# Attention and expert layer on one core: the first transposes of a pair moved behind a product for the maxima and a score group

## The chip, the cores and the metric

The kernel runs on one core of a Trainium2 chip. The metric is the device time in microseconds of one execution: the median of several runs, lower is better. The matrix engine is called TensorE (PE in the profile, its weight loads PEld), the others VectorE (DVE), ScalarE (ACT), GpSimd (POOL) and SyncE (SP, which issues most transfers). PSUM is the memory that TensorE writes; VectorE and ScalarE read it.

## The reference

Masked attention over 4 batches of 8 heads (768 positions, 64 features), followed by a layer of 8 experts of which each token uses one. Cut to what matters:

```python
q_bucket = np.sum((np.einsum('bhsd,dk->bhsk', q, proj) > 0) * 2 ** np.arange(6), axis=-1)
k_bucket = ...                                   # the same of k
mask = q_bucket[:, :, :, None] == k_bucket[:, :, None, :]
scores = np.where(mask, scale * np.matmul(q, k.transpose(0, 1, 3, 2)), -1000000000.0)
attn = np.exp(scores - scores.max(-1, keepdims=True))
attn = attn / (attn.sum(-1, keepdims=True) + 1e-09)
x = np.matmul(attn, v)                           # then tokens by 512 features
e_idx = np.argmax(x @ w_gate + modality_bias[modality_id], axis=1)
out[mask_e] = gate_w[mask_e, None] * (np.maximum(x[mask_e] @ w1[e], 0.0) @ w2[e])
```

A query sees only the keys with the same six sign bits. The kernel finds out by a product which queries have no such key at all (they average over all values).

## The kernel before, in words

The 32 heads are worked on as 16 pairs, numbered 0 to 15. The attention part is one loop over pairs with six steps each (`kt` 0 to 5, one for each block of 128 keys). Several pairs are in work at once, and in pair i's six steps TensorE does:

- **scores of pair i** (`score`, lines 309 to 328; letter S, or f to k of the table's tail). For each step three groups: head 0 on 512 queries, head 1 on 512 queries, both heads on the remaining 256. A group is one or two pairs of products (L306 and L307) into a `psum` tile of pool `ps_s` (called pss in the profile), of which there are two; ScalarE then takes the exponential (L319 for the first two groups, L324 for the third) into a buffer `pb`. GpSimd adds the exponentials up (L327).
- **maxima for pair i + 1** (`maxp`, lines 228 to 264; letter M). Products L240 (one query block on 512 keys) and L246 (two query blocks on the other 256 keys), into two tiles of pool `ps_m` (psm); VectorE reduces them (L242, L248). After some of them the maxima go through a transpose (`maxp_back`, L269, letter B) into a tile of pool `ps_x` (psx), which VectorE reads three times: L271 for each head, and L272, which marks the queries without a key in `lone`.
- **preparing pair i + 2** (letter T): `turn` (lines 172 to 197) transposes q and k in six groups of four (L181) into a psx tile each, which ScalarE copies out (L185); behind the second and third group of a head SP issues a transfer that shifts a half (L194, L196). Then `signs` (L208, read by VectorE, L210) and `patterns` (L223, read by VectorE or ScalarE, L224 and L225). That makes twelve pieces of work, of which eleven stand in one pair's six steps and the last (letter P) in the first step of the next pair.
- **the weighted sum of values** (`weigh`, lines 330 to 349; letter A): eight products (L342) a step, running two steps behind the scores, into tiles psu.

Beside these, `split` (letter W, L162 to L168, on ScalarE, VectorE and GpSimd) parts pair i + 3's loaded q and k into high and low parts for the transposes, `vadds` and `vsums` (v and V; L287 on TensorE, a psx tile) prepare the mean of the values, `sums` (Q, L360) adds up the softmax sums, and `finish`, `finish_x` and `route` (letters e to h, E to G, k, x, y) turn a finished batch of four pairs into gate logits, routing tables and stored rows; they fall into pairs 4 to 15 and differ from pair to pair. In pairs with i % 4 == 2 they put L409, L412, L590 and L592 on VectorE in the first steps, and L423 and L425 (rows of x, through a psx tile).

Pool `ps_x` has two tiles only, and all of L181, L208, L223, L269, L287, L360, L423 and others take the next of the two in turn. At the start of a pair the order of takers is: L269 of `maxp_back` (end of the pair before), L223 of letter P, and then the first transposes L181, which thus get the tile of L269 and need it free of L272.

What sets the order of the work is a table written by hand. TensorE's instructions are recorded under a manual schedule, in the order of the letters of `PLAN`; the other engines' instructions are put into order by a scheduler that uses an instruction-cost estimate. The loop reads one string a step:

```python
for kt in range(NT):
    for c in PLAN[kt]:
        if c == "S":
            next(ss)
        elif c == "M":
            next(ms, None)
        elif c == "T":
            next(ts, None)
        elif c == "P":
            next(last, None)
```

After the last pair the second part begins, in which the experts' weights are loaded, split into high and low parts (L755, L757) and multiplied with gathered token rows (L792 to L794, L834 to L836). The diff does not touch it.

Of the kernel before, what the change touches and what calls it, by code (L numbers as in the profile page):

```python
# [27 lines left out]

LAG = 2
PLAN = (  # L30
    "LvSPMTMSASfMTMfexyhk",
    "SMTVMSASfMTMeyghk",
    "SMTMSAQFGlSMTMEfxyk",
    "SMSATWSBMEekk",
# [947 lines left out]
```

## Time and profile before

| | before |
|---|---|
| median of three runs | 882.26 us (877.72, 884.44, 882.26) |
| the profiled execution | 876.72 us |
| its span, first to last instruction | 874.9 us |
| mean granted TensorE clock | 0.985 |
| start of a pair (its first L240): pairs 1, 2, 3, 4 | 64.60, 94.38, 124.12, 153.86 us |
| the same: pairs 5, 6, 7, 8 | 186.06, 218.37, 250.92, 283.38 us |
| the same: pairs 9, 10, 11, 12 | 315.62, 347.94, 380.27, 412.75 us |
| the same: pairs 13, 14 | 445.62, 477.60 us |
| TensorE's first instruction of the second part (L780) | 535.73 us |

A row of the timeline has the start in us from the span's start, the length in us, the engine, the source line, the operation, out<-in by the program's names, the shape and the count of instructions merged; a bracket names the engine's idle time ahead and what ended it. Matmuls overlap, so that the next one's start lies ahead of the drawn end of the one before, and a row's length is not what it costs: the distance between starts is. A row of the list of waits has who waited for whom, the total in us, how often, and the longest. Only the time for which TensorE waits sets the pace; the other engines' idle time says how much room they have.

### The profile page before, as it was taken

To read this page: it belongs to the slowest core of one execution; us is meant where nothing else is said; L and a number is where in the kernel's file an instruction comes from. 1 tells how busy PE (TensorE), PEld (TensorE's weight loads), DVE (VectorE), ACT (ScalarE), POOL (GpSimd) and SP (SyncE) were. 2 spreads that over 40 slices of the span, in tenths; PEclk is the share of its full clock that TensorE was granted. 3 is DMA by queue.
4 is the path that set the end of the run, shared out by engine and by line. 5 is a ranking of instruction groups with operands and counts; after the bars stand their busy time and mean duration, and the time that the engine had idled before them with its cause. 6 is when DMAs were issued, how large, how long until landed. Compare 5 with 4: busy or idle time off the path is not lost.

```text
span 874.9 us, 14548 instructions
## 1 busy us (share of the span) xinstructions
PE 817.9 (93%) x5154; PEld 579.5 (66%) x5154; DVE 585.8 (67%) x1029; ACT 506.0 (58%) x953; POOL 458.6 (52%) x347
## 2 busy tenths in 40 slices
PE   6799999999999999999999898879999999999993
PEld 3556555555555654555554555779999999998993
DVE  6776676676967676977677876954656565657550
ACT  4566666665666665666665464444555555557551
POOL 5387678657669857669757687322222221123010
PEclk9899999999999999999999999999999999999997
DMA  6423213212325221324210164796777777778750
GB/s 170 116 67 84 70 34 85 74 47 62 98 61 97 74 64 45 99 66 72 55 46 10 31 229 121 166 253 199 235 223 215 232 220 215 221 230 276 228 158 22
DMA packets 76753, 110.87 MB, mean 127 GB/s; under 512 B 10495, under 2 KB 52095, under 8 KB 76672
## 3 DMA queue, kind: packets, MB, share of 16 engines
q1 hardware_dynamic: 70880, 95.14, 39.2%
q0 software_dynamic: 4928, 13.14, 4.1%
q10 hardware_dynamic: 864, 1.57, 0.9%
q8 instruction: 43, 0.70, 0.4%
q14 instruction: 38, 0.31, 0.1%
HBM read 84.83 MB, written 13.33 MB: 112 GB/s over the span
## 4 chain that ended last, share of the span: by engine, by line
PE 74%; DVE 11%; DMA 4%; ACT 4%; issue 3%; POOL 2%; SPq 0%; POOLq 0%; DVEq 0%; ACTq 0%
PE psu L342 13%; PE pss L306 8%; PE pss L307 6%; PE yps L834 5%; PE yps L836 5%; PE yps L835 5%; PE psm L240 5%; PE hps L794 4%; PE hps L793 4%; PE hps L792 4%; PE psx L181 3%; PE psx L208 3%; PE psm L246 3%; POOL sp L327 2%; DVE mx L242 1%
## 5 line engine op out<-in xcount | busy, mean ns | idle before, releaser
L327 POOL TENSOR_TENSOR sp<-sp,pb 128x768 f32<-128x768 f32 x124 | 225.5, 1844 | 43.6 <-ACT pb L324 42.1
L757 DVE TENSOR_TENSOR w<-raw,w 128x1024 fp32r<-128x1024 f32 x108 | 134.9, 1251 | 94.4 <-ACT w L755 93.7
L755 ACT CAST w<-raw 128x1024 fp32r<-128x1024 f32 x112 | 117.1, 1048 | 61.9 <-PE yps L836 55.3
L242 DVE TENSOR_REDUCE mx<-psm 128x1 f32<-128x512 f32 x192 | 127.9, 686 | 32.0 <-PE psm L240 28.1
L342 PE MATMUL psu<-pb,vt 128*64 128x512 f32 (+1 forms) x768 | 145.6, 500 | 0.0
L319 ACT ACTIVATE pb<-pss 128x512 f32<-128x512 f32 x192 | 114.9, 599 | 40.6 <-PE pss L307 30.1
L324 ACT ACTIVATE pb<-pss 128x512 f32<-128x512 f32 x96 | 57.5, 599 | 127.1 <-PE pss L307 121.6
L792 PE MATMUL hps<-xh,w 128*128 128x256 f32 x384 | 108.9, 284 | 2.6 <-issue 1.6
L793 PE MATMUL hps<-xl,w 128*128 128x256 f32 x384 | 108.9, 284 | 0.0
L794 PE MATMUL hps<-xh,w 128*128 128x256 f32 x384 | 108.5, 283 | 0.0
L342 PEld LDWEIGHTS psu<-pb,vt 128*64 128x64 f32 x768 | 46.8, 136 | 86.4 <-issue 86.1
L769 POOL DMA_INDIRECT xg<-x_d,tb x26 | 31.6, 1214 | 124.6 <-DMA tb<-tab 99.5
L842 POOL DMA_INDIRECT out<-y,tb x26 | 34.5, 1328 | 117.7 <-ACT y L841 61.0
L834 PE MATMUL yps<-w,hl 128*128 128x512 f32 x208 | 83.4, 401 | 1.3 <-DVE hl L822 1.3
L836 PE MATMUL yps<-w,hh 128*128 128x512 f32 x208 | 81.8, 393 | 0.0
L835 PE MATMUL yps<-w,hh 128*128 128x512 f32 x208 | 81.6, 393 | 0.0
L248 DVE TENSOR_REDUCE mx<-psm 128x2 f32<-128x512 f32 x96 | 66.1, 689 | 22.9 <-PE psm L246 21.5
L306 PE MATMUL pss<-m_0g,s_0g 128*128 128x512 f32 x192 | 78.0, 406 | 0.0
L792 PEld LDWEIGHTS hps<-xh,w 128*128 128x128 f32 x384 | 73.4, 192 | 3.9 <-issue 1.8
L793 PEld LDWEIGHTS hps<-xl,w 128*128 128x128 f32 x384 | 73.6, 192 | 1.7 <-issue 1.2
L794 PEld LDWEIGHTS hps<-xh,w 128*128 128x128 f32 x384 | 73.5, 192 | 0.0
L167 POOL TENSOR_TENSOR n<-qk,n 128x384 fp32r<-128x384 f32 x36 | 40.2, 1122 | 56.9 <-ACT n L163 48.0
(214 smaller groups left out, 1767.3 us busy)
## 6 DMA issues: line engine op xcount, KB each, us to landing
raw<-moe_w SPq DMA_DIRECT2D x112, 512.0 KB
qk<-q SPq DMA_DIRECT2D x32, 192.0 KB
qk<-k SPq DMA_DIRECT2D x32, 192.0 KB
vt<-v SPq DMA_DIRECT2D x16, 384.0 KB
x_d<-xs SPq DMA_DIRECT2D x18, 256.0 KB
m_1g<-m_1g SPq DMA_DIRECT2D x16, 192.0 KB
s_1g<-s_1g SPq DMA_DIRECT2D x16, 192.0 KB
m_0g<-m_0g SPq DMA_DIRECT2D x15, 192.0 KB
```

Of the source, the lines that this page charges most:

```text
L242: nc.vector.tensor_reduce(out=mx[:, qt + j, hi, 0:1], in_=mp, axis=AX.X, op=ALU.max)
L306: nc.tensor.matmul(out, t["s1"][h][:, ks], t["m1"][h][:, cs], start=True, stop=False)
L327: (nc.vector if h and i in CFG["spd"] else nc.gpsimd).tensor_tensor(out=t["sp"][:, h], in0=(t["pb"][0] if kt == 1 else t["sp"])[:, h], in1 ...
L342: nc.tensor.matmul(t["u"][part][64 * h:64 * h + 64, 0:w], t["v"][:, h, kt], t["pb"][kt][:, h, COLS[part]], start=False, stop=(kt == NT - 1 ...
L755: nc.scalar.copy(out=hi, in_=r)
L757: (nc.gpsimd if pool else nc.vector).tensor_tensor(out=lo, in0=r, in1=hi.bitcast(F32), op=ALU.subtract)
L792: nc.tensor.matmul(hps, lo[:, c, fs], xh[:, c], start=(c == 0), stop=False)
L793: nc.tensor.matmul(hps, hi[:, c, fs], xl[:, c], start=False, stop=False)
L794: nc.tensor.matmul(hps, hi[:, c, fs], xh[:, c], start=False, stop=(c == 3))
L834: nc.tensor.matmul(yps[g], hl[fc][:, gs], hi[:, fb], start=(fc == 0), stop=False)
L835: nc.tensor.matmul(yps[g], hh[fc][:, gs], lo[:, fb], start=False, stop=False)
L836: nc.tensor.matmul(yps[g], hh[fc][:, gs], hi[:, fb], start=False, stop=(fc == 7))
```

## The change

The first string of the table is written anew. The letters T (four transposes) and M, S (the second product for the maxima, the score group of head 1) change places in the first step of every pair; all else stays.

```diff
 PLAN = (
-    "LvSPMTMSASfMTMfexyhk",
+    "LvSPMMSTASfMTMfexyhk",
     "SMTVMSASfMTMeyghk",
```

Pairs 0 to 13 have transposes in this step (for pair i + 2); in pairs 14 and 15 the letter T finds no work, and nothing changes.

On TensorE, at the start of pair 1 (which transposes pair 3's n_709; psm is a product for the maxima, pss the scores, psu the weighted sum):

```order
 L223 LDWEIGHTS pat
 L223 MATMUL psx<-bits_172,pat 128x384
-L240 MATMUL psm<-s_0g_113,m_0g_111 128x512
-L181 MATMUL psx<-identr,n_709 128x128 x4
-L240 MATMUL psm<-s_0g_113,m_0g_111 128x512
+L240 MATMUL psm<-s_0g_113,m_0g_111 128x512 x2
 L306 MATMUL pss<-m_1g_101,s_1g_103 128x512
 L307 MATMUL pss<-m_1g_105,s_1g_107 128x512
+L181 MATMUL psx<-identr,n_709 128x128 x4
 L342 MATMUL psu_652<-pb_178,vt 64x512 x2
```

The transposes now stand behind the second product and head 1's score group, and right ahead of the weighted sum.

On ScalarE, at the same place (L319 and L324 are exponentials, L185 the copy of the transposed q, L225 the last piece of the patterns):

```order
 L225 ACTIVATE s_0g_113<-psx 64x384
 L324 ACTIVATE pb_179<-pss 128x2x256
-L319 ACTIVATE pb_180<-pss 128x512
+L319 ACTIVATE pb_180<-pss 128x512 x2
+L225 ACTIVATE s_1g_114<-psx 64x384
 L185 CAST m_0g_126<-psx 128x512
-L225 ACTIVATE s_1g_114<-psx 64x384
-L319 ACTIVATE pb_180<-pss 128x512
 L324 ACTIVATE pb_180<-pss 128x2x256
 L185 CAST m_0g_126<-psx 128x256
```

The exponential of head 1's score group, which stood behind the copy and the pattern, is now ahead of both, and the copy comes last of the three.

On VectorE the order changes in pairs 6 and 10 alone. There, before, behind the reductions of the first step (L242 and L248 are reductions of the maxima; L409, L412, L590, L592 and L594 lead to the gate logits; L425 writes a row block of x):

```order
L409 TENSOR_TENSOR gl<-gn,rin 128x384
L412 TENSOR_REDUCE lg<-gl 128x48
L590 TENSOR_TENSOR l<-lg,bias 128x48
L592 TENSOR_REDUCE rm<-l 128x6
L248 TENSOR_REDUCE mx_3858<-psm 128x2
L242 TENSOR_REDUCE mx_3858<-psm 128x1
L425 TENSOR_TENSOR xs<-psx,rin 128x512
L242 TENSOR_REDUCE mx_3858<-psm 128x1
L594 TENSOR_TENSOR rd<-l,rm 128x48
```

And in the changed program at the same place:

```order
L409 TENSOR_TENSOR gl<-gn,rin 128x384
L412 TENSOR_REDUCE lg<-gl 128x48
L248 TENSOR_REDUCE mx_3858<-psm 128x2
L242 TENSOR_REDUCE mx_3858<-psm 128x1
L425 TENSOR_TENSOR xs<-psx,rin 128x512
L242 TENSOR_REDUCE mx_3858<-psm 128x1
L590 TENSOR_TENSOR l<-lg,bias 128x48
L248 TENSOR_REDUCE mx_3858<-psm 128x2
```

The two small operations L590 and L592 no longer stand ahead of the reductions; L592 and L594 follow later still. GpSimd's and SP's instructions keep their order.

## The prediction

> **What bounds the kernel now.** First the page's totals, the chain that ended last, the waits of TensorE and one pair's window (us; after the window, its length, then busy time and instructions by engine, granted clock, DMA share, GB/s).
>
> ```profile
> PE 817.9 (93%) x5154; PEld 579.5 (66%) x5154; DVE 585.8 (67%) x1029; ACT 506.0 (58%) x953; POOL 458.6 (52%) x347
> ...
> PE 74%; DVE 11%; DMA 4%; ACT 4%; issue 3%; POOL 2%; SPq 0%; POOLq 0%; DVEq 0%; ACTq 0%
> ...
> 124.12:153.86 29.74, 29.20 (x184) 17.13 (x184) 20.00 (x36) 20.05 (x43) 22.27 (x15) 1.00 0.25 67
> ...
> PE psx L181 <- DVE lone L272: 6.4, 12, 0.5
> PE psm L240 <- DVE mx L242: 3.7, 2, 2.0
> ```
>
> TensorE sets the time: it carries 74% of the chain, and in pair 3 it works 29.20 of 29.74 us at full clock, while no other engine passes 22.3. So the question is what its queue, which the plan writes in a fixed order, stands still for. The largest wait of the loop over pairs is the one that this change touches: transposes (L181) waiting for VectorE's last reader of a psx tile (L272), 12 times. Now the place itself, at the start of pair 4, TensorE alone, and the first and last of the twelve.
>
> ```profile
> 64.60 0.52 PE L240 MATMUL psm<-s_0g,m_0g 128*128 128x512 f32 x1
> 65.67 0.52 PE L181 MATMUL psx<-identr,n 128*128 128x128 f32 x4 [0.54 <-DVE lone L272]
> ...
> 153.86 0.52 PE L240 MATMUL psm<-s_0g,m_0g 128*128 128x512 f32 x1
> 154.92 0.50 PE L181 MATMUL psx<-identr,n 128*128 128x128 f32 x4 [0.54 <-DVE lone L272]
> 155.26 0.46 PE L240 MATMUL psm<-s_0g,m_0g 128*128 128x512 f32 x1
> 155.56 0.39 PE L306 MATMUL pss<-m_1g,s_1g 128*128 128x512 f32 x1
> 155.79 0.40 PE L307 MATMUL pss<-m_1g,s_1g 128*128 128x512 f32 x1
> 156.12 1.51 PE L342 MATMUL psu<-pb,vt 128*64 128x512 f32 x8
> ...
> 158.14 0.40 PE L246 MATMUL psm<-s_0g,m_0g 128*128 128x256 f32 x2
> 158.38 0.45 PE L181 MATMUL psx<-identr,n 128*128 128x128 f32 x4
> 158.67 0.47 PE L240 MATMUL psm<-s_1g,m_1g 128*128 128x512 f32 x1
> ...
> 413.82 0.51 PE L181 MATMUL psx<-identr,n 128*128 128x128 f32 x4 [0.54 <-DVE lone L272]
> ```
>
> Call the rows of pair 4 M1 (153.86), T (154.92), M2 (155.26), S2 (155.56 and 155.79) and A (156.12). T starts 1.06 us after M1. The bracket counts 0.54 of that as idle because M1 is drawn with a modelled end; the true loss shows beside a pair that doesn't wait, pair 13, and beside pair 14, which has no T left:
>
> ```profile
> 445.62 0.53 PE L240 MATMUL psm<-s_0g,m_0g 128*128 128x512 f32 x1
> 446.00 0.45 PE L181 MATMUL psx<-identr,n 128*128 128x128 f32 x4
> ...
> 447.14 1.08 PE L342 MATMUL psu<-pb,vt 128*64 128x512 f32 x4
> ...
> 477.60 0.75 PE L240 MATMUL psm<-s_0g,m_0g 128*128 128x512 f32 x2
> 478.19 0.40 PE L306 MATMUL pss<-m_1g,s_1g 128*128 128x512 f32 x1
> 478.43 0.40 PE L307 MATMUL pss<-m_1g,s_1g 128*128 128x512 f32 x1
> ```
>
> In pair 13 T follows M1 after 0.38 us, so each of the twelve waits costs 1.06 - 0.38 = 0.68 us. M1 to A is 2.26 us in pair 4 and 1.52 in pair 13.
>
> **The change part by part.** It removes no instruction and adds none: M2 and S2 go ahead of T in pairs 0 to 13, and A now follows T. Four costs have to be worked out.
>
> *The new start of a pair on TensorE.* Pair 14 runs M1, M2, S2 without T: S2 comes 0.59 us after M1, its second half 0.24 later. A product followed by T takes 0.24 (158.14 to 158.38). T is thus reached 0.59 + 0.24 + 0.24 = 1.07 us after M1. The tile it needs allowed a start at 1.06 in the old order, and nothing ahead of VectorE's release moves. Work of 0.69 us now fills a hole of 0.68, and the wait goes to almost nothing. From T to A no row exists. Below: T to a product is 0.29 (158.38 to 158.67). Above: 0.34 after a T that has waited (154.92 to 155.26), plus 0.10, which A costs more than a product behind S2 (0.33 against 0.23): 0.44. M1 to A is then 1.36 to 1.51; I take 1.45, nearer the upper end, since T arrives just as its tile is freed. Against 2.26 that gains **0.81 us a pair, bounds 0.75 to 0.90**.
>
> *What M2, S2 and T may now wait for.* The readers in pair 4, VectorE and then ScalarE:
>
> ```profile
> 154.35 0.42 DVE L272 TENSOR_SCALAR lone<-psx 128x256 fp32r<-128x256 f32 x1
> 154.81 0.55 DVE L224 CAST m_1g<-psx 64x384 fp32r<-64x384 f32 x1
> 155.39 1.29 DVE L242 TENSOR_REDUCE mx<-psm 128x1 f32<-128x512 f32 x2
> 158.58 0.69 DVE L248 TENSOR_REDUCE mx<-psm 128x2 f32<-128x512 f32 x1 [1.90 <-PE psm L246]
> ...
> 153.50 0.60 ACT L324 ACTIVATE pb<-pss 128x512 f32<-128x512 f32 x1
> 154.08 0.60 ACT L319 ACTIVATE pb<-pss 128x512 f32<-128x512 f32 x1
> 155.46 0.59 ACT L185 CAST m_0g<-psx 128x512 fp32r<-128x512 f32 x1 [0.79 <-PE psx L181]
> 156.07 0.49 ACT L225 ACTIVATE s_1g<-psx 64x384 fp32r<-64x384 f32 x1
> ```
>
> M2 takes the other psm tile, as in pair 14, where the same two products stand in a row. S2 needs the pss tile that ScalarE's L324 leaves at 154.10; it arrives at 153.86 + 0.59 = 154.45, 0.35 us later. It costs nothing, and if that exponential slipped by 0.60, one more operation of ScalarE, S2 would stand 0.25 us with T and A queued behind it.
>
> *What follows on the other engines.* On ScalarE S2's exponential now stands ahead of L225 and of T's copy L185. S2 ends near 155.09, so the three end at about 155.7, 156.2 and 156.8, where T's copy ended at 156.05. The first to want either psx tile is the second group of transposes, at 158.38 - 0.81 = 157.57, and its tile is the one of L225: 1.3 us to spare. The copy of this first group issues no DMA; those that shift halves (L194, L196 on SP) come after the second and third group, keep their order, and move up with TensorE. VectorE's reductions at 155.39 don't move; its idle 1.90 us ahead of L248 shrinks to 1.09. GpSimd's adds wait for exponentials and move up too.
>
> *Pairs 6 and 10,* where VectorE has routing work in that idle time, VectorE and then TensorE:
>
> ```profile
> 222.55 0.91 DVE L412 TENSOR_REDUCE lg<-gl 128x48 f32<-128x384 f32 x1
> 223.49 0.21 DVE L590 TENSOR_TENSOR l<-lg,bias 128x48 f32<-128x48 f32 x1
> 223.86 0.68 DVE L248 TENSOR_REDUCE mx<-psm 128x2 f32<-128x512 f32 x1
> 225.06 0.68 DVE L425 TENSOR_TENSOR xs<-psx,rin 128x512 f32<-128x512 f32 x1
> 225.88 0.46 PE L287 MATMUL psx<-va,ones 128*128 128x128 f32 x2 [0.49 <-DVE xs L425]
> ```
>
> There VectorE is the later one: L248 starts as soon as the small operations end, and TensorE waits for L425. TensorE's lead would be lost in full, but the changed program also puts L590 and L592 behind the three reductions and L425, so that L248 can start at 223.49 instead of 223.86. These two pairs gain 0.37 each, not 0.81. `oh`, for which those small operations work, is read by TensorE only in the next pair.
>
> **The sum:** ten pairs by 0.81 = 8.1; pairs 6 and 10, 0.74; pairs 0 and 13, which didn't wait, 0.07 each (1.52 to 1.45): 9.0 us. The bounds are 10 x 0.75 + 0.7 = 8.2 and 12 x 0.90 + 0.2 = 11.0. The profiled execution took 876.72 (span 874.9 and 1.8 around it) and would take 867.7. It stands 5.5 below the median of the three runs, 882.26; against that median the forecast is **873.3 us**, 1.0% less.
>
> **The rivals.**
>
> *VectorE takes the gain back everywhere (877.8).* If all twelve pairs behaved like pair 6, the gain would be 12 x 0.37 = 4.4 us. For it: VectorE's chain at the pair's start is not shortened. Against it: the 1.90 us of idle time ahead of L248 exceed the 0.81.
>
> *The change does nothing for the time (882.3).* T's tile is released no earlier, so the wait might only be renamed, standing ahead of A or reappearing at S2. Against it: M2 and S2 have what they need, by the rows above, and are the length of the hole.
>
> *Slower, by the port between VectorE and GpSimd (896).* VectorE's subtraction L167 runs twice a pair, once alone and once beside GpSimd's adds (L327):
>
> ```profile
> 161.91 0.56 DVE L167 TENSOR_TENSOR n<-qk,n 128x384 fp32r<-128x384 f32 x1
> 205.21 1.09 DVE L167 TENSOR_TENSOR n<-qk,n 128x384 fp32r<-128x384 f32 x1 [1.39 <-issue]
> 154.24 3.60 POOL L327 TENSOR_TENSOR sp<-sp,pb 128x768 f32<-128x768 f32 x2 [0.92 <-ACT pb L324]
> 202.26 3.62 POOL L327 TENSOR_TENSOR sp<-sp,pb 128x768 f32<-128x768 f32 x2 [0.37 <-ACT pb L324]
> ```
>
> Beside the adds of 202.26 it idles 1.39 us and takes 1.09, 1.92 more than alone. Were the early one (161.91) caught too, at a place where TensorE waits for all of it, twelve pairs would pay 23.0 us and save 9.0: 896. It decides from the point where the last adds of the pair before, which end at 157.84, reach L167, which moves up to 161.1; 3.3 us are missing. The Trainium skill says the same of the mechanism ("SBUF — State Buffer", Who interferes with whom: a VectorE instruction with two SBUF inputs and a GpSimd instruction that reads SBUF take one port as an exclusive lock, and the second blocks until the first is done). The trace agrees so far: L167 ends at 206.30, after the adds' end at 205.88. By that rule alone an instruction could stand for both adds, 3.6 us, and the sum for twelve pairs would be 43 - 9 = 34 us slower; by the rows, which show it clear of the adds, the term is nothing.
>
> **How the numbers follow.** Forecast 0.80; VectorE 0.10; nothing 0.05; slower 0.05. About 1% (8.8 us) is what a measurement of this kernel can tell from no change, and a gain of 9.0 lies on that line: of the forecast's 0.80 I put 0.46 beyond it and 0.34 within. With the two middle rivals that gives faster 0.46, same 0.49, slower 0.05. For the range, the upper bound of the gain (871.3) with the 4.5 us by which the lowest run before lay under its median gives 866.8; the VectorE case (877.8) with the 2.2 us by which the highest lay above gives 880.0. The two rivals beyond it hold a tenth.
>
> **What would show it right or wrong.** Right: the wait of L181 for L272 falls from 6.4 us to under 1; M1 to A is near 1.45; pairs 1 to 3 shrink from 29.74 to 28.9; pairs 6 and 10 still show L287 waiting for L425, and longer than 0.49. Wrong: S2 waiting for L324, or T still waiting 0.5 behind S2; pairs that keep their length because L240 or L246 now wait for a reduction; a second L167 of over 1 us in a pair.

## The result, and the profile after

The changed kernel took 870.83 us (median of 869.06, 871.29, 870.83) against 882.26 us: a ratio of 0.990, 95% interval 0.985 to 0.995. Two later comparisons, in five rounds each and on two different chips, gave 0.9948 (0.9922 to 0.9974) and 0.9892 (0.9852 to 0.9931). All three intervals lie below 1, so the change shortens the time, by 0.5 to 1.1%; why the size is so uncertain is told below. Single executions at a clearly lower clock (one of before's took 1124.81 us at 0.654, the profiled one of r8_ddpd 912.24 at 0.844) or over 1.5% above their kernel's fastest are left out of every ratio and of the medians below. The profiled execution took 869.06 us (span 867.3, granted clock 0.982) where before's took 876.72 (874.9, 0.985).

The page's totals, the chain's shares, pair 3's window and three of TensorE's waits in the changed kernel:

```profile
PE 817.1 (94%) x5154; PEld 580.9 (67%) x5154; DVE 585.7 (68%) x1029; ACT 506.5 (58%) x953; POOL 458.9 (53%) x347
...
PE 75%; DVE 7%; DMA 5%; issue 4%; POOL 4%; ACT 4%; SPq 0%; POOLq 0%; ACTq 0%; DVEq 0%
...
123.76:152.78 29.02, 29.02 (x185) 17.24 (x184) 20.01 (x36) 20.07 (x43) 22.27 (x15) 1.00 0.26 69
...
PE psm L240 <- DVE mx L242: 3.7, 2, 2.0
...
PE psx L287 <- DVE xs L425: 1.5, 3, 0.5
...
PE psm L246 <- DVE mx L242: 1.4, 3, 0.6
```

The wait of L181 for L272, 6.4 us before, has left the list. VectorE's share of the chain fell from 11 to 7%, and in pair 3 TensorE is busy for the whole 29.02 us. Grown is L246's wait for L242, from 0.2 us once to 1.4 in three waits, 0.6 at most. The start of pair 4 on TensorE:

```profile
152.78 0.75 PE L240 MATMUL psm<-s_0g,m_0g 128*128 128x512 f32 x2
153.37 0.40 PE L306 MATMUL pss<-m_1g,s_1g 128*128 128x512 f32 x1
153.60 0.40 PE L307 MATMUL pss<-m_1g,s_1g 128*128 128x512 f32 x1
153.84 0.50 PE L181 MATMUL psx<-identr,n 128*128 128x128 f32 x4
154.28 1.51 PE L342 MATMUL psu<-pb,vt 128*64 128x512 f32 x8
```

T starts 1.06 us after M1, as before, but without a bracket: the two products and S2 have filled the time. M1 to A is 1.50 us, where before had 2.26. The same place on VectorE and ScalarE:

```profile
153.27 0.42 DVE L272 TENSOR_SCALAR lone<-psx 128x256 fp32r<-128x256 f32 x1
...
156.74 0.69 DVE L248 TENSOR_REDUCE mx<-psm 128x2 f32<-128x512 f32 x1 [1.14 <-PE psm L246]
...
154.12 0.60 ACT L319 ACTIVATE pb<-pss 128x512 f32<-128x512 f32 x1 [0.53 <-PE pss L307]
154.74 0.49 ACT L225 ACTIVATE s_1g<-psx 64x384 fp32r<-64x384 f32 x1
155.25 0.59 ACT L185 CAST m_0g<-psx 128x512 fp32r<-128x512 f32 x1
```

VectorE still has 1.14 us in hand ahead of L248, and nobody on TensorE waits for ScalarE's three operations.

From one pair's first L240 to the next one's, before and after:

| pairs | before | after |
|---|---|---|
| 1, 2, 3 | 29.78, 29.74, 29.74 | 28.99, 28.97, 29.02 |
| 4, 5, 7, 8, 9 | 32.20, 32.31, 32.46, 32.24, 32.32 | 31.47, 31.56, 31.69, 31.50, 31.53 |
| 11, 12 | 32.48, 32.87 | 31.69, 32.11 |
| **6, 10** | 32.55, 32.33 | **32.70, 32.46** |
| **13** | 31.98 | **33.53** |

Ten pairs lose 0.72 to 0.79 us each, 7.6 in all. Pairs 6 and 10 became longer, and so, in this execution, did pair 13.

### The profile page after: what moved, and what is told of

It is laid out like the page before. It is cut to its first block, busy times and chain, and to the rows that moved or that the text cites. A ratio compares the mean times of both kernels' runs of the same rounds, so it can differ in the third digit from the quotient of the medians.

```text
span 867.3 us, 14548 instructions
## 1 busy us (share of the span) xinstructions
PE 817.1 (94%) x5154; PEld 580.9 (67%) x5154; DVE 585.7 (68%) x1029; ACT 506.5 (58%) x953; POOL 458.9 (53%) x347
## 3 DMA queue, kind: packets, MB, share of 16 engines
q10 hardware_dynamic: 864, 1.57, 0.9%
## 4 chain that ended last, share of the span: by engine, by line
PE 75%; DVE 7%; DMA 5%; issue 4%; POOL 4%; ACT 4%; SPq 0%; POOLq 0%; ACTq 0%; DVEq 0%
PE psu L342 13%; PE pss L306 8%; PE pss L307 6%; PE psm L240 5%; PE yps L834 5%; PE yps L836 5%; PE yps L835 5%; PE hps L794 4%; PE hps L793 4%; PE hps L792 4%; PE psx L208 3%; PE psx L181 3%; PE psm L246 3%; POOL sp L327 2%; DVE mx L242 1%
## 5 line engine op out<-in xcount | busy, mean ns | idle before, releaser
L327 POOL TENSOR_TENSOR sp<-sp,pb 128x768 f32<-128x768 f32 x124 | 225.7, 1844 | 45.8 <-ACT pb L324 44.3
L242 DVE TENSOR_REDUCE mx<-psm 128x1 f32<-128x512 f32 x192 | 127.8, 686 | 33.4 <-PE psm L240 30.7
L319 ACT ACTIVATE pb<-pss 128x512 f32<-128x512 f32 x192 | 114.9, 599 | 47.7 <-PE pss L307 37.4
L324 ACT ACTIVATE pb<-pss 128x512 f32<-128x512 f32 x96 | 57.5, 599 | 122.1 <-PE pss L307 113.3
L248 DVE TENSOR_REDUCE mx<-psm 128x2 f32<-128x512 f32 x96 | 66.1, 689 | 15.7 <-PE psm L246 14.3
L306 PE MATMUL pss<-m_1g,s_1g 128*128 128x512 f32 x192 | 68.0, 354 | 0.7 <-ACT pb L324 0.6
```

The source lines that it names most:

```text
L242: nc.vector.tensor_reduce(out=mx[:, qt + j, hi, 0:1], in_=mp, axis=AX.X, op=ALU.max)
L306: nc.tensor.matmul(out, t["s1"][h][:, ks], t["m1"][h][:, cs], start=True, stop=False)
L327: (nc.vector if h and i in CFG["spd"] else nc.gpsimd).tensor_tensor(out=t["sp"][:, h], in0=(t["pb"][0] if kt == 1 else t["sp"])[:, h], in1 ...
```

## The experiments

In the three kernels that double L272, line numbers behind it are higher by one (L273, L307, L343).

**The changed kernel again (r1_after, r9_after_again),** without an edit.

> The changed kernel again, in five rounds, to size the gain. Theory: the hole of 0.68 us in twelve pairs is filled, ten pairs keep 0.7 to 0.8 us each and pairs 6 and 10 get nothing, so about 7.5 us less than before (0.9915 of it). In the profile M1 to A is 1.49 to 1.51 us in the twelve pairs again, and pairs 6 and 10 are again 0.1 to 0.2 us longer than the 32.55 and 32.33 us of before. Rival (the 11.4 us between the first medians is the gain, so something beyond the hole is won): 0.987.

> The changed kernel a second time, beside the three that follow, to size its gain on another set of runs. From the pairs' lengths: 10 x 0.77 less, 2 x 0.14 more, 7.4 us; from the first repetition 5 us, with a mean granted clock that was lower than that of before by 0.0024, which is 2 us. Theory (the lower clock belongs to the change): 5 us again, and a mean clock of all its runs about 0.002 below before's. Rival (the clock scatters from one batch of runs to the next): 7 us and the same clock.

Measured: 871.62 against 876.45 us, and 871.17 against 881.02. M1 to A is 1.49 to 1.51 in both profiles, pairs 6 and 10 take 32.73 and 32.49, 32.68 and 32.46. The mean clock of all runs was 0.9828 against 0.9852 in the first batch, 0.9845 against 0.9827 in the second: the difference changes its sign from batch to batch, so the theory in r9's expectation, that the lower clock belongs to the change, fell. Multiplying each run's time by its clock gives means of 856.4 against 863.4 us, and 858.2 against 865.6: gains of 7.0 and 7.4, where the plain means say 5.0 and 9.2. That takes the whole time to scale with the clock; by the slope within before's runs, 0.72 us for each 0.001 in the first batch and 0.60 in the second, the gains would be 6.7 and 8.1. The pairs' lengths give 7.6 - 0.28 + 0.05 (pair 13 in r1_after, 31.93) = 7.4, and need no such scaling. The standard error of these clocked means is 0.3 to 1.0 us.

**T behind M2 alone (r2_half).**

```diff
-    "LvSPMMSTASfMTMfexyhk",
+    "LvSPMMTSASfMTMfexyhk",
```

> T moves behind the second product M2 only, not behind the score group S2. Theory of the filled hole: T still can't start before 1.06 us after M1 (the release by L272), M2 fills 0.24 to 0.30 of the hole, and behind T come S2 and A as before: M1 to A about 1.95 us where before has 2.26 and the change 1.50, so the gain is about 0.31 us a pair, 3 us in all, and the wait of L181 for L272 stays with about 12 x 0.25 us. Rival (not the filling counts but that T stands apart from M1, or that M2 right behind M1 is cheaper): M1 to A near 1.5 and the whole gain of 7.5 us.

Measured: 875.47 us, 0.9994 of before (0.9966 to 1.0022). Pair 4 on TensorE:

```profile
152.84 0.76 PE L240 MATMUL psm<-s_0g,m_0g 128*128 128x512 f32 x2
153.90 0.52 PE L181 MATMUL psx<-identr,n 128*128 128x128 f32 x4 [0.31 <-DVE lone L272]
...
154.88 1.51 PE L342 MATMUL psu<-pb,vt 128*64 128x512 f32 x8
```

T starts at 1.06 once more, with a wait of 0.31, and M1 to A is 2.04 (2.02 to 2.04 in the twelve pairs): 0.23 a pair gained, what one product costs, where 0.31 was expected. The hole shrinks by what is put into it, and by nothing else. Over the whole kernel ten such gains less 0.27 lost in each of pairs 6 and 10 (32.83, 32.59) are 1.8 us, below what these runs can tell.

**T behind A as well (r3_behind_a).**

```diff
-    "LvSPMMSTASfMTMfexyhk",
+    "LvSPMMSATSfMTMfexyhk",
```

> T moves one place further, behind the weighted sum A as well. Theory: with S2 ahead of T the hole is filled already (no wait of L181 is left), so A ahead of it wins nothing more: M1 to A about 1.15 us, from M1 to the third score group about 2.9 us as in the change, the same time as the change within 0.1%. In pairs 6 and 10 VectorE's routing operations stand a little differently, 0.3 us at most. Rival (T arrives just as its tile is freed and still loses 0.1 to 0.2 us there, which the brackets don't show): 1 to 2 us faster than the change.

Measured: 870.59 us, 0.9929 of before (0.9905 to 0.9953), 1.0 us below r1_after's median, which these runs can't tell from nothing or from the rival's 1 to 2. The trace can. Pair 4:

```profile
152.93 0.75 PE L240 MATMUL psm<-s_0g,m_0g 128*128 128x512 f32 x2
...
154.08 1.51 PE L342 MATMUL psu<-pb,vt 128*64 128x512 f32 x8
155.52 0.53 PE L181 MATMUL psx<-identr,n 128*128 128x128 f32 x4
155.89 0.35 PE L306 MATMUL pss<-m_0g,s_0g 128*128 128x256 f32 x1
```

From M1 to the third score group it takes 2.96 us, the change 2.94 (152.78 to 155.72). Pairs 1 to 3 take 28.98, 28.96 and 28.97, and pairs 1 to 12 together are 0.2 us shorter than in r1_after. Once T no longer waits, its place is worth nothing more.

**The same L272 done twice, in before, in the change, and with T behind A (r5_before_twice, r6_after_twice, r7_behind_a_twice).**

```diff
-        nc.vector.tensor_scalar(out=t["lone"][rows, cs], ...)
+        for _ in range(2 if n == 2 and len(heads) == 2 else 1):
+            nc.vector.tensor_scalar(out=t["lone"][rows, cs], ...)
```

> The kernel before, in which VectorE does L272 of the second head twice (the same values into the same tile), so that the tile for T comes free about 0.45 us later (from the start of one L272 to the next instruction it is 0.46). Theory (TensorE stands at T for the release by L272 and pays every bit of it): T starts 1.5 us after M1 instead of 1.06, the wait of L181 for L272 goes from 6.4 to about 11.5 us, M1 to A from 2.26 to 2.70, and 12 x 0.45 = 5.4 us are added to the time of before. Rival (the idle time at T is only how the matmuls are drawn, or is taken up further on): less than 2 us.

> The changed kernel with the same L272 done twice. Theory (M2 and S2 fill the hole exactly, 0.69 us of work for 0.68, so nothing is in reserve): T arrives 1.07 us after M1, its tile is free at 1.5, the wait of L181 for L272 is back with about 0.43 us in each of twelve pairs, and about 5 us are added to the time of the change. Rival (behind M2 and S2 T has reserve): no wait comes back and at most the 0.45 us of pairs 6 and 10, where VectorE is late, are added, 1 us.

> T behind A as well, with the same L272 done twice. Theory: T arrives 2.6 us after M1 there, 1.1 us after its tile is free even so, so the ten ordinary pairs keep their length of 28.97 and 31.5 us and no wait of L181 for L272 shows; only pairs 6 and 10, where VectorE is late, get up to 0.45 us longer: 1 us more than the same kernel with one L272. Rival (the doubled L272 delays VectorE's reductions, and these hold up TensorE, whatever T does): 5 us more, as in the changed kernel.

Measured: 893.11 (1.0208 of before, 1.0160 to 1.0255), 878.39 (1.0020, 0.9994 to 1.0046) and 872.57 us (0.9958, 0.9933 to 0.9983). The changed kernel with two L272, VectorE and TensorE:

```profile
154.38 0.42 DVE L273 TENSOR_SCALAR lone<-psx 128x256 fp32r<-128x256 f32 x1
154.84 0.55 DVE L224 CAST m_1g<-psx 64x384 fp32r<-64x384 f32 x1
155.42 0.42 DVE L273 TENSOR_SCALAR lone<-psx 128x256 fp32r<-128x256 f32 x1
...
155.99 0.50 PE L181 MATMUL psx<-identr,n 128*128 128x128 f32 x4 [0.88 <-DVE lone L273]
```

The second one was put behind L224, so the tile comes free 1.04 us later and not 0.45: the size expected was wrong, the comparison holds with 1.04. In before T starts 2.11 us after M1 instead of 1.06, and pairs 1 to 3 grow from 29.74 to 30.79, by 1.05. In the change T starts at 2.10, and they grow from 28.99 to 30.04, again by 1.05: **nothing was in reserve**. With T behind A they take 28.97 to 29.00: the late tile costs nothing there. Twelve times 1.05 is 12.6 us, and r5_before_twice is 16.9 slower. The rest goes with its clock, 0.978 on the mean of its six runs against 0.984 for before's: in its profile the clock is at half for a while in pairs 6, 7, 11 and 13 (the last section tells more), in the first three behind T's wait, now 1.58 us; before's profile has no such stretch in pairs 1 to 13.

Pairs 6 and 10 don't fit this account. In the change with two L272 they grow by only 0.13 and 0.16, to 32.83 and 32.62 (the two stretches of the table at the end of this section are 7.30 and 3.52 us in pair 6 there, and with the table's 22.0 give 32.82). With T behind A they grow by 2.0 each, to 34.70 and 34.51. Pair 6 of the latter, VectorE, GpSimd and TensorE (L591, L595 and L328 are L590, L594 and L327 in the other kernels):

```profile
223.62 1.02 DVE L591 TENSOR_TENSOR l<-lg,bias 128x48 f32<-128x48 f32 x1
224.91 1.61 DVE L595 TENSOR_TENSOR rd<-l,rm 128x48 f32<-128x48 f32 x1
226.45 1.27 DVE L242 TENSOR_REDUCE mx<-psm 128x1 f32<-128x512 f32 x2
...
223.15 1.42 POOL L167 TENSOR_TENSOR n<-qk,n 128x384 fp32r<-128x384 f32 x1 [4.91 <-ACT n L163]
224.65 3.58 POOL L328 TENSOR_TENSOR sp<-pb,pb 128x768 f32<-128x768 f32 x2
...
227.18 0.64 PE L246 MATMUL psm<-s_0g,m_0g 128*128 128x256 f32 x2 [2.00 <-DVE mx L242]
```

The order on VectorE has changed once more. L591 and L595 end at 224.64 and 226.52, just behind GpSimd's L167 (224.57) and the first of its two L328 (226.46). L246 starts 12.69 us after M1, 0.51 later than with one L272. The other 1.5 us come behind it, where the clock is at half from 227.38 to 230.79. Pair 12 takes 0.5 to 0.6 us more than this account gives in each of the three kernels, as its L385, too, waits for VectorE, 1.25 us instead of the 0.74 of before's L384.

**Pairs 6 and 10 with the old first step (r4_old_6_10).**

```diff
-                for c in PLAN[kt]:
+                for c in "LvSPMTMSASfMTMfexyhk" if kt == 0 and i in (6, 10) else PLAN[kt]:
```

> The change, but pairs 6 and 10 keep the old first step, and with it VectorE's old order there. Theory (the moved L592 and L594 meet GpSimd's L167, and what they lose there delays L242 and TensorE's L246): pairs 6 and 10 come back to 32.55 and 32.33 us, and the L594 that takes 0.98 us takes 0.20 again; 0.3 us less than the change in all, too little for the time of the whole, to be read from the pairs' lengths. Rival (those two pairs are longer for another reason, such as what the pairs before them hand over): they stay at 32.7 and 32.5 us or grow by the 0.5 us that the new start of the pair saves.

Measured: 868.48 us, 0.9926 of before (0.9894 to 0.9958). Pairs 6 and 10 take 32.56 and 32.34, as in before, and the rest is as in the change. To see why, pair 6 in the changed kernel, VectorE, then GpSimd, then TensorE:

```profile
223.59 0.69 DVE L248 TENSOR_REDUCE mx<-psm 128x2 f32<-128x512 f32 x1 [0.17 <-PE psm L246]
224.32 0.46 DVE L294 TENSOR_TENSOR vs<-psx,vs 32x64 fp32r<-32x64 f32 x2
224.81 0.56 DVE L167 TENSOR_TENSOR n<-qk,n 128x384 fp32r<-128x384 f32 x1
225.28 0.19 DVE L592 TENSOR_REDUCE rm<-l 128x6 f32<-128x48 f32 x1
225.51 0.98 DVE L594 TENSOR_TENSOR rd<-l,rm 128x48 f32<-128x48 f32 x1
...
227.25 1.29 DVE L242 TENSOR_REDUCE mx<-psm 128x1 f32<-128x512 f32 x2
...
225.41 1.02 POOL L167 TENSOR_TENSOR n<-qk,n 128x384 fp32r<-128x384 f32 x1 [5.83 <-ACT n L163]
...
222.85 0.46 PE L287 MATMUL psx<-va,ones 128*128 128x128 f32 x2 [0.49 <-DVE xs L425]
...
227.99 0.50 PE L246 MATMUL psm<-s_0g,m_0g 128*128 128x256 f32 x2 [0.56 <-DVE mx L242]
```

and in before, VectorE and GpSimd:

```profile
226.61 0.69 DVE L248 TENSOR_REDUCE mx<-psm 128x2 f32<-128x512 f32 x1 [0.17 <-PE psm L246]
...
228.78 0.73 DVE L603 TENSOR_TENSOR oh<-rw,rwm 128x48 bf16<-128x48 f32 x1
...
229.66 1.29 DVE L242 TENSOR_REDUCE mx<-psm 128x1 f32<-128x512 f32 x2
...
228.44 1.02 POOL L167 TENSOR_TENSOR n<-qk,n 128x384 fp32r<-128x384 f32 x1 [6.34 <-ACT n L163]
```

L287 comes 7.04 us after M1 (before 7.51): the forecast gain is there, 0.47. But L592 and L594 now stand between L248 and L242, and that stretch of VectorE grew from 3.05 to 3.66 us; TensorE's L246 waits at its end. Both orders have one small subtraction or comparison of two SBUF tiles held until GpSimd's L167 ends, L594 for 0.98 us here, L603 for 0.73 in before, where each takes 0.20 alone. In r4_old_6_10 L594 takes 0.20 as expected, but L603 takes 0.74 in its place: the expectation had overlooked it. Of the 0.61, the two moved operations make up some 0.45 by their own steps and the longer stay at the port 0.25 (0.78 beyond the 0.20 instead of 0.53); the other order of the three behind them gives 0.1 back.

**L167 of pairs 9 and 13 on VectorE (r8_ddpd, r10_ddpd_again, r12_before_ddpd, r11_behind_a_ddpd).**

```diff
-                e = (... "PPPP" if i in CFG["rq"] else CFG["sub"])[2 * h + x]
+                e = (... "PPPP" if i in CFG["rq"] else "DDPD" if i in (9, 13) else CFG["sub"])[2 * h + x]
```

> The changed kernel, in which GpSimd's subtraction L167 of the split for pairs 9 and 13 (it falls into pairs 6 and 10) goes to VectorE. Theory (in pairs 6 and 10 VectorE's L594 stands in the port behind GpSimd's L167, 0.98 us instead of 0.20, and TensorE's L246 waits 0.56 us for L242 behind it): VectorE pays one more L167 of 0.48 and saves 0.78 at L594; its order also changes there, L601, L613 and L603 (0.7 us together) fall behind the reductions. L594 takes 0.20 us, the wait of L246 for L242 is gone in both pairs, and these shrink from 32.70 and 32.46 us by at least 0.5 each, to 32.1 and 31.9 or less; about 1.2 us for the whole. Rival (VectorE's amount of work, not the port, makes these pairs late): one more L167 makes them longer, 32.9 us or more.

> The changed kernel with L167 of pairs 9 and 13 on VectorE instead of GpSimd, once more, for a profile at full clock. Theory of the port: as put before; L594 takes 0.20 us, L246 doesn't wait for L242 in pairs 6 and 10, and these take 32.1 and 31.9 us or less against 32.70 and 32.46; 1.2 us less than the change in all. Rival (the amount of VectorE's work decides): 32.9 us or more.

> The kernel before with L167 of pairs 9 and 13 on VectorE alone, to see whether that edit needs the change. VectorE's order in pairs 6 and 10 becomes the same as in the change with this edit (L590 behind three reductions; L592, L594 and L599 behind the two L167; L601, L613 and L603 last). Theory (these pairs are set by VectorE from one reduction to the next, not by where T stands): pairs 6 and 10 come to the same lengths as with the change, about 32.1 and 31.9 us against 32.55 and 32.33, and the ordinary pairs stay at 29.74 and 32.2 to 32.5; 0.9 us less than before. Rival (TensorE's 0.8 us of lead count there as well): they stay 0.5 us or more above those of the change with this edit.

> Both together: T behind A (which gives T a reserve of 1.5 us) and L167 of pairs 9 and 13 on VectorE. No computation is left out. Theory: ordinary pairs as in the change (28.97 and 31.5 us), pairs 6 and 10 at 32.1 and 31.9; the same time as the change with L167 on VectorE alone, 1.2 us below the change and 8 to 9 us below before by the pairs, and the best of all versions if anything is. Rival (T behind A hands its delay to ScalarE's copies and to the exponentials of pairs 6 and 10): those two pairs gain nothing.

Measured: 868.93 us (0.9898 of before, 0.9859 to 0.9937) and 872.35 (0.9900, 0.9860 to 0.9940) for the change with this edit, 878.45 (0.9973, 0.9942 to 1.0004) for before with it, and 870.05 (**0.9881**, 0.9843 to 0.9920) for both edits together. The change with the edit (r10_ddpd_again), VectorE and TensorE in pair 6:

```profile
225.07 0.69 DVE L248 TENSOR_REDUCE mx<-psm 128x2 f32<-128x512 f32 x1 [0.17 <-PE psm L246]
...
226.29 1.12 DVE L167 TENSOR_TENSOR n<-qk,n 128x384 fp32r<-128x384 f32 x2
...
227.56 0.21 DVE L594 TENSOR_TENSOR rd<-l,rm 128x48 f32<-128x48 f32 x1
...
228.04 1.29 DVE L242 TENSOR_REDUCE mx<-psm 128x1 f32<-128x512 f32 x2
...
228.78 0.50 PE L246 MATMUL psm<-s_0g,m_0g 128*128 128x256 f32 x2
```

With no L167 on GpSimd there L594 takes 0.21 us and L246 has no bracket. VectorE has more to do, and the pairs are shorter, 32.00 and 31.79 us: the port and the order decide, not the amount of work. r12's premise didn't hold (in its trace L590 and L592 stayed ahead of the reductions), and its pairs, 32.41 and 32.24, lie 0.41 and 0.45 above those of the change with the edit, nearer its rival. Pair 6 in five kernels, in us:

| | M1 to L287 | L248 to L242 | sum | pair 6 | pair 6 less the sum |
|---|---|---|---|---|---|
| before | 7.51 | 3.05 | 10.56 | 32.55 | 21.99 |
| the change | 7.04 | 3.66 | 10.70 | 32.70 | 22.00 |
| the change, old step in 6 and 10 | 7.52 | 3.05 | 10.57 | 32.56 | 21.99 |
| the change, L167 on VectorE | 7.06 | 2.97 | 10.03 | 32.00 | 21.97 |
| before, L167 on VectorE | 7.52 | 2.91 | 10.43 | 32.41 | 21.98 |

Two stretches explain the pair's length to 0.03 us. The version with both edits has the lowest ratio of all and a reserve for T (29.00 us in pairs 1 to 3; 31.98 and 31.77 in 6 and 10), but its 1.4 us over the change are too little for these runs to show.

## Why the prediction was right, and where it was not

- **The hole and its filling: right.** T was to arrive 1.07 us after M1 at a tile free at 1.06; it starts at 1.06 without a wait. T to A was the open term, 0.29 to 0.44, and is 0.44, the upper bound: M1 to A 1.50 against the forecast 1.45, 0.76 a pair against 0.81, within 0.75 to 0.90. That S2 needs to be in front too (r2_half), and that more doesn't help (r3_behind_a), is shown.
- **S2, ScalarE, the other tiles: right.** S2 waits for nothing. The three operations of ScalarE end 1.94, 2.45 and 3.06 us after M1, 0.1 later than worked out; L248's idle time is 1.14 (forecast 1.09).
- **Pairs 6 and 10: wrong, and in sign.** Forecast 0.37 less each, measured 0.15 and 0.13 more. The step that failed: the prediction let L590 and L592 move behind the reductions at no price, because `oh`, for which they work, is read only in the next pair. The gain came, 0.47 us at L287, but the stretch from L248 to L242 behind it grew by 0.61. That `oh` is read later is so, and beside the point: what counts is who is queued behind them on VectorE, and that is L242, for which TensorE's L246 waits. That L592 and L594 follow later still was known from the order of the program; where they landed wasn't priced. The sign "L287 still waits, longer than 0.49" also failed: the bracket stayed 0.49, the rest shows ahead of an L240.
- **The rival with the port: the mechanism is real here, with another instruction.** Not twelve L167 at 1.92 us, but L594 in two pairs at 0.78. The Trainium skill ("SBUF — State Buffer", Who interferes with whom) says that a VectorE instruction with two SBUF inputs contends with a GpSimd instruction that reads SBUF for a shared port, and that this port is an exclusive lock. The trace agrees: GpSimd's L167 starts at 225.41, L594 at 225.51, and they end at 226.43 and 226.49.
- **The rivals "VectorE takes it back" and "nothing": refuted** by L248's idle time and by the pairs' lengths.
- **The sum: 7.4 us by the pairs, against 9.0.** Of the 1.6 too much, 1.0 is pairs 6 and 10, 0.5 is T to A, and 0.1 is pairs 0 and 13, forecast 0.07 each: pair 13 gave 0.05, and pair 0 nothing (25.64 in r1_after, 25.63 before). The difference between the two profiled executions, 7.66, is not that sum: the half-clock stretches (below) cost the later one some 2.7 us more in the loop (1.2 ahead of pair 1, 1.5 in pair 13), and it was 2.7 us faster from the first L780 on, in the part that the diff doesn't touch. That part took 334.9 us in r2_half's profile and 342.9 in r9_after_again's.
- **The time: 873.3 forecast, 870.8, 871.6 and 871.2 measured.** It is nearer than the sum deserves, and that is partly luck. The term that was off is the base, before's median: 882.26 in the first three runs, then 876.45 over 31, 876.22 over 22 and 881.02 over 17 in the later batches, the last two on the same chip. The gain stood by the prediction on the line of what can be told from no change, about 1%; the three ratios, 0.5 to 1.1% less, lie on both sides of it.

## What to carry to other kernels

A stall of an engine with a fixed order is worth what stands behind it and is ready, up to the length of the stall; measure the hole from start to start, and fill it with a little more than its length, since a filling of exactly its length leaves no reserve. Where a scheduler orders the other engines, price each instruction that it moves by who is queued behind it, not only by who reads its result. And read a gain of 1% from the stretches that the change touches: there it can be told to some hundredths of a us, in the whole time it can't.

## What the runs showed of the hardware

TensorE's granted clock falls to half for 3.41 us at a time, at the same place in some executions and not in others of the same kernel. Two neighbouring windows of that length around the same wait in pair 13, before and then the change (the last figure but two is the granted clock):

```profile
459.50:462.91 3.41, 2.65 (x21) 1.53 (x13) 3.27 (x10) 1.92 (x4) 2.88 (x4) 1.00 0.02 5
462.91:466.32 3.41, 2.21 (x11) 0.97 (x11) 2.50 (x5) 1.12 (x2) 2.30 (x2) 1.00 0.26 58
```

```profile
454.52:457.93 3.41, 1.44 (x12) 0.93 (x10) 3.34 (x10) 1.67 (x3) 2.96 (x3) 1.00 0.26 58
457.93:461.34 3.41, 3.41 (x9) 1.43 (x11) 1.30 (x3) 1.11 (x2) 1.09 (x1) 0.50 0.00 0
```

and the same instructions of pair 13 there, in before and in the change:

```profile
464.11 0.50 PE L240 MATMUL psm<-s_0g,m_0g 128*128 128x512 f32 x1 [1.96 <-DVE mx L242]
```

```profile
457.92 0.80 PE L240 MATMUL psm<-s_0g,m_0g 128*128 128x512 f32 x1 [1.97 <-DVE mx L242]
...
459.50 2.41 PE L342 MATMUL psu<-pb,vt 128*64 128x512 f32 x8
```

Both waited the same 1.96 us; in one the eight products that follow take 2.41 us instead of 1.51, and the pair 1.55 us more. Six of the thirteen profiles at full clock have it in this place, with 33.5 to 33.6 us for pair 13, and seven have not, with 31.9 to 32.0.

The traces also show when it happens. Within each profile, the half-clock stretches ahead of 560 us start whole multiples of 3.413 us apart (in the change's at 21.03, 38.09, 457.93 and 492.07 us) and are 3.41 us or a multiple of it long. The grid lies differently in each execution. In the six profiles the wait of pair 13 falls whole into one step of the grid; in the seven others an edge cuts it, in the first two windows above into 0.76 and 1.20 us, and no step there holds more than 1.74 us of idle time as drawn. From 60 to 545 us, all nine steps with 1.95 us or more of idle time were followed by half clock and none with less than 1.57; between these, both happened.

The Trainium skill ("TensorE: Matmul & The Clock Gate", Part 1) says that the clock is set from windows of 3.4 us that run free of the kernel. The grid agrees. By the same part the clock falls after a whole idle window; here 1.95 us of idle time in one window was enough.
